# Row scatters issued two at a time inside the next group, and other PSUM banks, in a chained attention and expert kernel

## The chip, the cores and the metric

The kernel runs on one core of a Trainium2 chip. Its engines are TensorE (PE, with PEld for its weight loads), VectorE (DVE), ScalarE (ACT), GpSimd (POOL) and SyncE (SP), which only issues DMA here. The metric is the device time in microseconds. Before the change it is 1347.3 us, the median of three runs (1346.11 to 1347.62).

## The reference, cut to what matters

```
def reference(**kwargs):
    attn_out = _attn_ref(...)                 # pooled-key attention, 8 batches, 8 heads, 576 x 64
    x = attn_out.transpose(0, 2, 1, 3).reshape(4608, 512)
    x = _moe_ref(x, expert_emb, tau, w1, w2)  # each token to one of 8 experts
    return _moe2_ref(x, w1, w2, w3, w_out)

def _moe2_ref(x, w1, w2, w3, w_out):          # 4608 tokens, d_model 512, d_ff 1024
    a = x @ w1
    b = x @ w2
    h = a * b @ w3
    return (h @ w_out).astype(np.float32)
```

All is float32. The change is in the last function, the last stage of the kernel, and at its seam to the experts. The kernel has multiplied w3 and w_out into one 1024 x 512 matrix earlier, which is `wph` and `wpl` here.

## The kernel before, in words

Every float32 product is made of three products of rounded halves: a value is cast to a high half (ScalarE), the low half is the difference (VectorE or GpSimd), and `mm3` or `product` multiplies high by high, high by low and low by high. Operands in the profile end in h and l for that reason.

The expert stage (class `Moe`) sorts tokens by expert into 43 slots of 128 rows. 36 blocks always run. The rest are in nested conditional code (`single`, line 1533 ff., the branch is line 1541); each engine reads the number of used slots and skips what isn't needed. Here 37 blocks run, so one conditional block is entered and the others are skipped. Block j puts its output product in PSUM bank 5, 6 or 0 by `j % 3` (`mm2`, line 1515 ff.).

The last stage (class `Moe2`) works on the tokens in five groups: the first 512 tokens as the plain group, then four groups of 1024. Its weights w1 and w2 are read in 8 blocks, once for every group, as `w32` tiles of 512 KB from DRAM (`wload`, line 1678), two buffers.

- Plain group: `plain(k)`, k from 0 to 7, makes two products of 12 matmuls each into two PSUM banks, multiplies them and splits the result. Then `outp` makes four output tiles of 128 rows (24 matmuls each), ScalarE copies them to SBUF (line 1999), and four row scatters follow.
- Each later group: `pair(k)`, k from 8 g to 8 g + 7, treats 2 x 512 tokens in the manner of Strassen's scheme: 7 products of 6 matmuls, so 42 matmuls a pair. It needs sums of the weights, which GpSimd makes two pairs ahead (`wsums`, four operations, lines 1686 to 1689), and splits the next pair's weights in three pieces (`wpieces`, line 1713): ScalarE casts all three, VectorE makes the low half of two, and GpSimd that of the middle one. After these the load of the weights three pairs ahead is issued, which takes the buffer that the pieces just read.
- After the fourth pair of a group come 8 output products whose results ScalarE copies to the tiles o0 to o7 (line 2018); after the eighth come 8 more, which VectorE adds to them (line 2032). Between the latter the tokens of the next group are prepared (`prep`, `step`, `flip_in`). Then all 8 tiles are scattered, except that the last group scatters each tile as soon as it is summed.
- `scatter` (lines 1905 to 1915) is a one-element memset and one indirect DMA, both on GpSimd: 128 rows of 512 values go to the rows that `idx` names. `idx[g]` is filled by `flip_out` (line 1742) while group g - 1 runs.

The order on each engine is that of the Python code (`manual_schedule`): instructions are issued as the loops call them, and each waits on semaphores for its operands and for the buffers that it overwrites. PSUM has 8 banks of 128 x 512 values; a name `b0` to `b7` is one bank with one buffer. Pair k uses banks 0 to 2 if k is even and 3 to 5 if it is odd.

Of the kernel before, what the change touches and what calls it, by code (L numbers as in the profile page):

```python
# [10 lines left out]
I32 = mybir.dt.int32  # L11
# [5 lines left out]
P = 128  # L17
# [6 lines left out]
NT = N // P  # L24
# [37 lines left out]
def psum(c, bank, name):  # L62
    pool = c.psw if bank == 6 else c.ps
    return pool.tile([P, 512], F32, tag=f"b{bank}", name=name, bufs=1)
# [48 lines left out]
def mm3(nc, out, a, b, first, last):  # L113
    nc.tensor.matmul(out, a[0], b[0], start=first, stop=False)  # L114
    nc.tensor.matmul(out, a[0], b[1], start=False, stop=False)  # L115
    nc.tensor.matmul(out, a[1], b[0], start=False, stop=last)  # L116


class Fillers:
# [6 lines left out]
    def run(self, n):  # L126
        while n > 0 and self.q:
            self.q.pop(0)()
            n -= 1
# [1158 lines left out]
class Moe:  # L1288
# [226 lines left out]
    def mm2(self, j):  # L1515
        c, nc = self.c, self.c.nc
        hT = self.hT.pop(j)
        py = psum(c, (5, 6, 0)[j % 3], "py")
        for k in range(8):
            wh, wl = self.s2[k // 2]  # L1520
            mm3(nc, py, hT[k], (wh[:, k % 2, :], wl[:, k % 2, :]), k == 0, k == 7)
        self.py[j] = py
# [103 lines left out]
class Moe2:  # L1626
# [102 lines left out]
    def flip_out(self, g, ch):  # L1729
        nc = self.c.nc  # L1730
        y = self.y.pop((g, ch))
        T = self.st().rearrange("p (q t n) -> p q t n", q=4, t=2)
        for t in range(2):
            nc.vector.transpose(  # L1734
                T[:, :, t].rearrange("p q (k i) -> p q k i", k=4),
                y[:, t, :DM].rearrange("p (k q i) -> p q k i", k=4, q=4),
            )
        nc.sync.dma_start(out=self.c.scr2[ch], in_=T.rearrange("p q t n -> p q (t n)"))
        if ch == 0:
            self.idx[g] = self.wpool.tile([P, 8], I32, tag="idx", name="idx", bufs=2)  # L1740
        to = self.idx[g][:, 2 * ch:2 * ch + 2] if g == 0 else self.idx[g].rearrange("p (h c) -> p c h", h=2)[:, ch]
        nc.vector.tensor_copy(to, y[:, :, DM])

# [79 lines left out]
    def plain(self, k):  # L1823
        c, nc = self.c, self.c.nc
        h, l = self.wh.pop(k)
        p = []
        for u in range(2):
            pp = psum(c, 2 * (k % 2) + u, "pab")
            for a in range(4):
                s = (2 * u + a // 2, slice(a % 2 * P, a % 2 * P + P))  # L1830
                mm3(
                    nc, pp, (h[:, s[0], s[1]], l[:, s[0], s[1]]), tuple(x[:, a, :] for x in self.x01),
                    a == 0, a == 3,
                )
            p.append(pp)
        if k + 1 < self.PLAIN:
            self.wsplit(k + 1)
            self.wload(k + 3)
        sa = self.tmp("pa", 2)
        nc.scalar.copy(sa, p[0])  # L1840
        nc.vector.tensor_tensor(sa, sa, p[1], op=ALU.mult)
        hi, lo = (x[:, k // 4 * 512:k // 4 * 512 + 512] for x in self.abtile(k % 4))
        nc.scalar.copy(hi, sa)
        nc.vector.tensor_tensor(lo, sa, hi.bitcast(F32), op=ALU.subtract)
# [50 lines left out]

    def outp(self, g, t, fs, base):
        c, nc = self.c, self.c.nc
        po = psum(c, (0, 1, 2, 6, 7, 0, 6, 7)[t], "po")
        for n, f in enumerate(fs):
            ah, al = self.abtile(f % 4)  # L1900
            s = slice(base(f, t), base(f, t) + P)
            mm3(nc, po, (ah[:, s], al[:, s]), (c.wph[:, f, :], c.wpl[:, f, :]), n == 0, n == len(fs) - 1)
        return po
# [63 lines left out]
    def run(self, pool):  # L1967
        c, nc = self.c, self.c.nc
        self.pool = pool
        self.todo = None  # L1970
        c.wph = pool.tile([P, 8, DM], F32R, name="wph")
        c.wpl = pool.tile([P, 8, DM], F32R, name="wpl")
        for k in range(self.PLAIN):
            self.plain(k)
            if k < 4:
                self.split_wp(k)
            if k < 2:
                self.load_wp(k + 2)
            if 3 <= k <= 6:
                self.flip_out(1, k - 3)  # L1980
            if 2 <= k <= 5:
                self.load_y(1, k - 2)
            if k == 5:
                self.flip_in(1, 0)
            if k == 6:
                self.flip_in(1, 1)
                self.wsums(8)
        self.flip_in(1, 2)
        pr = [self.prep(1, ch) for ch in range(3)]
        pr[0][0]()  # L1990
        pr[1][0]()
        self.wsplit(8)
        self.wload(10)
        for t in range(4):
            po = self.outp(0, t, range(8), lambda f, t: f // 4 * 512 + t * P)
            for i in self.ORDER[0][t]:
                self.step(0, i, pr)
            self.acc[t] = o = self.partial(t)
            nc.scalar.copy(o, po)
        for t in range(4):  # L2000
            self.scatter(0, t, self.acc[t])
        for g in range(1, self.PAIRS + 1):
            more = g < self.PAIRS
            for f in range(8):
                self.pair(8 * g + f, f < 7)
                if more:
                    if f in (1, 3, 5, 6):
                        self.flip_out(g + 1, (1, 3, 5, 6).index(f))
                    if f in (0, 2, 4, 5):
                        self.load_y(g + 1, (0, 2, 4, 5).index(f))  # L2010
                    if f >= 5:
                        self.flip_in(g + 1, f - 5)
                if f == 3:
                    self.finish()
                    for t in range(8):
                        po = self.outp(g, t, range(4), lambda f, t: t * P)
                        self.acc[t] = self.partial(t)
                        nc.scalar.copy(self.acc[t], po)
            if more:
                pr = [self.prep(g + 1, ch) for ch in range(3)]  # L2020
                pr[0][0]()
                pr[1][0]()
            self.finish()
            po = {}
            for t in range(8):
                po[t] = self.outp(g, t, range(4, 8), lambda f, t: t * P)
                if more:
                    for i in self.ORDER[1][t]:
                        self.step(g, i, pr)
                for x in ((), (0,), (1, 2), (3,), (4,), (5,), (6,), (7,))[t] if more else (t,):  # L2030
                    o = self.acc[x]
                    nc.vector.tensor_tensor(o, po[x], o, op=ALU.add)
                    if not more:
                        self.scatter(g, x, o)
            for t in range(8 if more else 0):
                self.scatter(g, t, self.acc[t])

    ORDER = (
        ("abuc", "defg", "hijw", ""),
# [152 lines left out]
```

## Time and profile before

| | |
|---|---|
| median of three runs | 1347.3 us |
| the profiled execution | 1343.8 us |
| its span, first to last instruction | 1342.0 us |
| mean granted TensorE clock | 0.951 |
| PE busy | 1226.2 us (91%), 6124 matmuls |
| DVE busy | 883.3 us (66%) |
| POOL busy | 567.8 us (42%) |
| ACT busy | 496.5 us (37%) |

The last stage runs from 752.5 us of the span to its end. Busy time of PE counts matmuls that overlap their successors, so a stop shows as idle time of PE only in the waits and the timeline. The granted clock is a share of 2.4 GHz; 0.5 is 1.2 GHz. Times in rows count from the span's start.

### The profile page before, as it was taken

The numbers are of one execution on the slowest core, as the hardware profiler recorded it, in microseconds if no ns is written. First come the engines' busy times: TensorE is split into PE (matmuls) and PEld (weight loads), VectorE is DVE, ScalarE is ACT, GpSimd is POOL, SyncE is SP. The second block draws the span as 40 slices with busy tenths as digits, with TensorE's granted clock in tenths as the row PEclk, the third lists the DMA queues.
The fourth block names the chain that finished last, engine by engine and source line by source line (L and its number), as shares of the span: only waits on it lengthen the run. The fifth ranks groups of instructions, "written<-read, shape, count | busy, mean of one in ns | idle before, by whom it ended". The sixth has DMA issues, their size and how long they took to land. (4 is left out here: it accounts for less than half of the span.)

```text
span 1342.0 us, 19906 instructions
## 1 busy us (share of the span) xinstructions
PE 1226.2 (91%) x6124; PEld 964.9 (72%) x6124; DVE 883.3 (66%) x1706; ACT 496.5 (37%) x897; POOL 567.8 (42%) x705
## 2 busy tenths in 40 slices
PE   7788789899799988989898898999999999999996
PEld 6565666677677766767676686788778777787885
DVE  5999998866476586566574375728664864686262
ACT  4655455432232232233231343434334433444330
POOL 2675666622042133122232138525842663376222
PEclk9779899999999989989898999999999999999998
DMA  9999996568988878778974273315221431332001
GB/s 244 253 236 255 248 245 204 196 188 251 282 255 263 232 244 248 233 209 253 265 211 131 78 235 85 115 36 157 94 95 58 131 126 63 110 102 87 16 16 63
DMA packets 115215, 228.66 MB, mean 170 GB/s; under 512 B 11720, under 2 KB 73160, under 8 KB 115088
## 3 DMA queue, kind: packets, MB, share of 16 engines
q1 hardware_dynamic: 105824, 197.75, 50.8%
q0 software_dynamic: 8832, 28.92, 6.7%
q8 instruction: 50, 0.82, 0.3%
q14 instruction: 77, 0.63, 0.2%
q10 hardware_dynamic: 432, 0.55, 0.1%
HBM read 292.39 MB, written 72.40 MB: 272 GB/s over the span
## 5 line engine op out<-in xcount | busy, mean ns | idle before, releaser
L1483 DVE SCALAR_TENSOR_TENSOR hTl<-U,hTh 128x128 fp32r<-128x128 f32 x288 | 81.2, 344 | 112.3 <-ACT hTh L1481 75.4
L115 PE MATMUL hp<-w1l,xTh 128*128 128x512 f32 x296 | 124.8, 422 | 19.0 <-DVEq L1379 15.9
L114 PE MATMUL hp<-w1h,xTh 128*128 128x512 f32 x296 | 124.1, 419 | 15.1 <-ACT w1h L1359 11.6
L1529 POOL DMA_INDIRECT ys<-y,sidx x37 | 37.5, 1013 | 201.9 <-DVE y L1528 138.5
L116 PE MATMUL hp<-w1h,xTl 128*128 128x512 f32 x296 | 122.1, 413 | 0.0
L116 PE MATMUL py<-w2h,hTl 128*128 128x512 f32 x296 | 118.1, 399 | 3.4 <-DVE hTl L1483 3.4
L1481 ACT ACTIVATE hTh<-U 128x512 fp32r<-128x512 f32 x72 | 45.3, 631 | 204.7 <-DMA U<-scr 109.0
L114 PE MATMUL py<-w2h,hTh 128*128 128x512 f32 x296 | 118.3, 400 | 2.6 <-ACTq L1385 2.5
L115 PE MATMUL py<-w2l,hTh 128*128 128x512 f32 x296 | 118.1, 399 | 1.0 <-DVEq L1385 1.0
L1713 DVE TENSOR_TENSOR wgl<-sum,wgh 128x1024 fp32r<-128x1024 f32 x32 | 44.4, 1388 | 109.3 <-ACT wgh L1709 109.3
L116 PE MATMUL po<-wph,abl 128*128 128x512 f32 x288 | 112.9, 392 | 0.8 <-DVE abl L1858 0.6
L115 PE MATMUL po<-wpl,abh 128*128 128x512 f32 x288 | 112.3, 390 | 0.0
L114 PE MATMUL po<-wph,abh 128*128 128x512 f32 x288 | 112.2, 390 | 0.0
L1811 PE MATMUL pst<-xsh,wgh 128*128 128x512 f32 x256 | 103.8, 405 | 3.2 <-ACT pc L1879 2.1
L1811 PE MATMUL pst<-xsl,wgh 128*128 128x512 f32 x256 | 102.9, 402 | 0.4 <-DVE xsl L1801 0.4
L1811 PE MATMUL pst<-xsh,wgl 128*128 128x512 f32 x256 | 102.6, 401 | 0.0
L1713 POOL TENSOR_TENSOR wgl<-w,wgh 128x512 fp32r<-128x512 f32 x32 | 44.9, 1405 | 127.2 <-ACT wgh L1709 125.4
L115 PEld LDWEIGHTS hp<-w1l,xTh 128*128 128x128 f32 x296 | 59.6, 202 | 39.7 <-DVEq L1379 20.9
L114 PEld LDWEIGHTS hp<-w1h,xTh 128*128 128x128 f32 x296 | 59.3, 200 | 31.7 <-ACT w1h L1359 13.4
L1857 ACT CAST abh<-pa 128x512 fp32r<-128x512 f32 x32 | 19.9, 621 | 150.3 <-DVE pa L1890 150.3
L1686 POOL TENSOR_TENSOR sum<-w 128x256 f32<-128x256 f32 x32 | 28.9, 904 | 101.0 <-DMA w<-wq 74.0
L116 PEld LDWEIGHTS hp<-w1h,xTl 128*128 128x128 f32 x296 | 59.7, 202 | 13.4 <-DVE xTl L76 0.4
(300 smaller groups left out, 3143.1 us busy)
## 6 DMA issues: line engine op xcount, KB each, us to landing
w2r<-in_moe_w_dram SPq DMA_DIRECT2D x152, 512.0 KB
w1r<-in_moe_w_dram SPq DMA_DIRECT2D x150, 512.0 KB
scr<-T SPq DMA_DIRECT2D x34, 768.0 KB
U<-scr SPq DMA_DIRECT2D x136, 192.0 KB
w<-wq SPq DMA_DIRECT2D x40, 512.0 KB
yin<-ys SPq DMA_DIRECT2D x36, 256.5 KB
qs<-in_q_dram SPq DMA_DIRECT2D x16, 576.0 KB
kv<-in_k_dram SPq DMA_DIRECT2D x32, 288.0 KB
```

Of the source, the lines that this page charges most:

```text
L114: nc.tensor.matmul(out, a[0], b[0], start=first, stop=False)
L115: nc.tensor.matmul(out, a[0], b[1], start=False, stop=False)
L116: nc.tensor.matmul(out, a[1], b[0], start=False, stop=last)
L1481: nc.scalar.activation(h4, u, ACTF.Relu)
L1483: nc.vector.scalar_tensor_tensor(l4[:, k], u[:, k], 0.0, h4[:, k].bitcast(F32), op0=ALU.max, op1=ALU.subtract)
L1529: nc.gpsimd.indirect_dma_start(out=self.ys, out_offset=bass.IndirectOffsetOnAxis(ap=c.sidx[:, j:j + 1], axis=0), in_=y, in_offset=None, bo ...
L1686: g.tensor_tensor(s[:, 0], b12, b11, op=ALU.subtract)
L1713: eng.tensor_tensor(l[:, s], src, h[:, s].bitcast(F32), op=ALU.subtract)
L1811: self.c.nc.tensor.matmul(out, ws[wi], x[xi], start=first and i == 0 and n == 0, stop=i == 1 and n == 2, skip_group_check=True,)
L1857: nc.scalar.copy(hi, pr)
```

## The change

The scatters of a group are no longer issued at its end. They are put in a list, `late`, and after each pair of the next group the first two of the list are issued: four pairs for eight scatters, two for the plain group's four. The row numbers `idx` get a third buffer. The last group's own scatters stay as they are.

The first plain block writes PSUM banks 6 and 7 in place of 0 and 1 (later even blocks still 0 and 1). The plain group's four output tiles are in banks 4 to 7 in place of 0, 1, 2 and 6. Expert blocks from number 36 on, the conditional ones, put their output product in bank 5 in place of 5, 6 or 0.

```diff
     def mm2(self, j):
-        py = psum(c, (5, 6, 0)[j % 3], "py")
+        py = psum(c, (5, 6, 0)[j % 3] if j < NT else 5, "py")
...
     def flip_out(self, g, ch):
-            self.idx[g] = self.wpool.tile([P, 8], I32, tag="idx", name="idx", bufs=2)
+            self.idx[g] = self.wpool.tile([P, 8], I32, tag="idx", name="idx", bufs=3)
...
     def plain(self, k):
-            pp = psum(c, 2 * (k % 2) + u, "pab")
+            pp = psum(c, (6 if k == 0 else 2 * (k % 2)) + u, "pab")
...
     def outp(self, g, t, fs, base):
-        po = psum(c, (0, 1, 2, 6, 7, 0, 6, 7)[t], "po")
+        po = psum(c, (4, 5, 6, 7)[t] if g == 0 else (0, 1, 2, 6, 7, 0, 6, 7)[t], "po")
...
     def run(self, pool):
             self.acc[t] = o = self.partial(t)
             nc.scalar.copy(o, po)
-        for t in range(4):
-            self.scatter(0, t, self.acc[t])
+        late = [(0, t) for t in range(4)]
         for g in range(1, self.PAIRS + 1):
             more = g < self.PAIRS
             for f in range(8):
                 self.pair(8 * g + f, f < 7)
+                for x in late[:2]:
+                    self.scatter(*x, self.acc[x[1]])
+                del late[:2]
                 if more:
...
                     if not more:
                         self.scatter(g, x, o)
-            for t in range(8 if more else 0):
-                self.scatter(g, t, self.acc[t])
+            late = [(g, t) for t in range(8 if more else 0)]
```

## Rows read from the trace of the kernel before

**Rows 1.** Waits of PE from 745 us on: total us, times, longest.
```profile
PE pst L1811 <- POOL wgl L1713: 10.0, 4, 3.8
PE pab L114 <- DVEq L1541: 3.5, 1, 3.5
...
PE pst L1811 <- ACT o L1999: 1.1, 1, 1.1
...
PE pst L1811 <- DVE xsl L1801: 0.4, 1, 0.4
```

**Rows 2.** Stretches of PE: from:to, length, busy (count), clock, DMA share, GB/s.
```profile
752.52:759.69 7.17, 7.17 (x25) 0.76 0.49 149
765.28:770.78 5.50, 5.50 (x26) 1.00 0.60 191
820.47:832.24 11.77, 10.26 (x43) 1.00 0.22 86
832.24:848.65 16.41, 12.66 (x44) 0.79 0.31 93
890.67:900.33 9.66, 9.66 (x43) 1.00 0.26 87
900.34:909.97 9.63, 9.63 (x44) 1.00 0.22 76
961.33:974.92 13.59, 11.51 (x44) 0.87 0.32 111
1214.94:1228.51 13.57, 11.49 (x43) 0.87 0.21 54
```

**Rows 3.** POOL in order of time, 943 to 990: start, us, ..., [idle before].
```profile
949.07 0.98 POOL L1908 DMA_INDIRECT out_dram<-o,idx  x1 [0.16 <-issue]
...
958.48 0.96 POOL L1908 DMA_INDIRECT out_dram<-o,idx  x1 [0.22 <-issue]
959.46 0.76 POOL L1686 TENSOR_TENSOR sum<-w 128x256 f32<-128x256 f32 x1
...
962.72 1.26 POOL L1713 TENSOR_TENSOR wgl<-w,wgh 128x512 fp32r<-128x512 f32 x1
967.86 0.80 POOL L1686 TENSOR_TENSOR sum<-w 128x256 f32<-128x256 f32 x1 [3.88 <-DMA w<-wq]
...
970.82 1.47 POOL L1713 TENSOR_TENSOR wgl<-w,wgh 128x512 fp32r<-128x512 f32 x1
975.91 0.74 POOL L1686 TENSOR_TENSOR sum<-w 128x256 f32<-128x256 f32 x1 [3.62 <-DVE pb L1892]
```

**Rows 4.** POOL in order of time, 820 to 846.
```profile
826.88 1.68 POOL L1908 DMA_INDIRECT out_dram<-o,idx  x1 [0.22 <-issue]
...
831.12 0.75 POOL L1686 TENSOR_TENSOR sum<-w 128x256 f32<-128x256 f32 x1
...
834.86 1.70 POOL L1713 TENSOR_TENSOR wgl<-w,wgh 128x512 fp32r<-128x512 f32 x1
```

**Rows 5.** ACT in order of time, 952 to 958.
```profile
955.15 0.63 ACT L1709 CAST wgh<-w 128x512 fp32r<-128x512 f32 x1
```

**Rows 6.** POOL in order of time, 1216 to 1240.
```profile
1225.13 1.29 POOL L1713 TENSOR_TENSOR wgl<-w,wgh 128x512 fp32r<-128x512 f32 x1
1230.26 1.13 POOL L1686 TENSOR_TENSOR sum<-w 128x256 f32<-128x256 f32 x1 [3.84 <-DVE abl L1858]
```

**Rows 7.** PE in order of time, 748.5 to 754.3.
```profile
752.52 0.47 PE L114 MATMUL pab<-xah,wgh 128*128 128x512 f32 x1 [3.51 <-DVEq L1541]
```

**Rows 8.** Line 1541's queue instructions, 744.9 to 752.6: ns min/median/max, first and last start.
```profile
L1541 PEldq COMPARE_BRANCH  x2: 193/1834/3475, 745.1 to 749.4; - x2
...
L1541 DVEq EVENT_SEMAPHORE  x2: 21/21/21, 752.4 to 752.5; - x2
```

**Rows 9.** DVE in order of time, 748 to 755.
```profile
753.57 1.23 DVE L1713 TENSOR_TENSOR wgl<-w,wgh 128x1024 fp32r<-128x1024 f32 x1 [3.71 <-ACT wgh L1709]
```

**Rows 10.** PE in order of time, 819.5 to 825.
```profile
824.02 0.50 PE L1811 MATMUL pst<-xsl,wgh 128*128 128x512 f32 x1 [0.40 <-DVE xsl L1801]
```

## The prediction

> **What bounds the kernel now.** I read the waits of TensorE over the last stage first, because the matrix engine is busy nearly throughout there and only what stops it can be won. Of its stops the large ones have two causes: four waits for the low half of a weight piece that GpSimd (POOL) writes, 10.0 us together with 3.8 us the longest, and one wait of 3.5 us for VectorE's queue ahead of the stage's first product [rows 1]. A third, 1.1 us, is for a copy out of PSUM, and 0.4 us follows it for an operand.
>
> Then I cut the stage into stretches that hold the same work, so that a stop and the slow clock behind it show as one difference [rows 2]. A pair of blocks (42 matmuls) takes 9.66 and 9.63 us where nothing stops it. Pair 9, the second after the plain group, takes 16.41 us; pair 17, the second of the next group, takes 13.59; pair 33 takes 13.57, and pair 25 between them is like them (three such pairs, the first and last shown). The first plain block takes 7.17 us where a later one takes 5.50. The granted clock says why these are longer than their stop: its mean is 0.76, 0.79 and 0.87 of full in the long stretches and 1.00 in the others. Each of these long stretches has a stop of 2.1 us or more at or just before its start (the three like ones (10.0 - 3.8) / 3 each); pair 8, whose stops are the 1.1 and 0.4 us, kept 1.00. So what a large stop costs is the stop and a stretch at 1.2 instead of 2.4 GHz behind it.
>
> Third, GpSimd's own order around such a stop [rows 3]. Eight scatters stand between the weight sums of one pair and those of the next: the first starts at 949.07 and the last at 958.48, and at 959.46 the sums start with no idle time at all before them. The piece that TensorE waits for starts at 962.72 and ends at 963.98; the pair that needs it had started at 961.33. GpSimd was simply still issuing scatters.
>
> **The scatters moved.** Removed from the start of each group: eight scatters, 949.07 to 959.44, 10.4 us of GpSimd, at three boundaries, and four after the plain group, which end just before the sums at 831.12 [rows 3, 4]. None is deleted; each comes back two at a time behind the piece that GpSimd writes in the first four pairs (in two pairs after the plain group).
>
> What is late next at a boundary: the sums can't start before the scatters' old place, 949.0, and must not start later than 959.46, which bounds the gain on that side at nothing. They take from 959.46 to 962.72, so from 949 they would be done near 953. The piece itself also needs ScalarE's cast, which starts at 955.15 and takes 0.63 [rows 5]. So it would start at about 955.8 and end at 957.1 by the 1.26 us of its row, 4.2 us before the pair starts at 961.33. The same kernel shows this case already: pairs 12 and 13 stand in the middle of a group, where no scatter stands ahead of their sums, and take 9.66 and 9.63 us [rows 2]. I take pair 13 as the model of pairs 17, 25 and 33: 3 x (13.59 - 9.63) with 13.57 for the last gives 11.9 us. Pair 9 after the plain group: 16.41 - 9.63 = 6.8 us. There the four scatters end and the sums start at 831.12, the piece starts at 834.86 and ends at 836.56, while pair 9 starts at 832.24. Four scatters at 1.34 us (below) are 5.4 us; begun that much earlier, it ends at about 831.2, 1 us ahead.
>
> What the scatters cost in their new place: after a piece GpSimd is idle 3.62 to 3.84 us until the next weights land [rows 3, 6], because the load of these waits for that very piece to free their buffer. One scatter is 1.34 us from start to start in the run of eight (949.07 to 958.48 over seven steps). Two are 2.7 us and fit. The bound on the other side is the slowest of all, 1.68 us [rows 4]; two such, with the 0.3 us each that memset and waiting add to the row's 0.96 or 0.98 (949.07 to 959.46 over eight), are 4.0 us, 0.4 over the hole. Behind the hole the piece still has room: pair 17's next piece ends at 972.29 against a pair start at 974.92 (2.6 us), and in the last group 1226.42 against 1228.51 (2.1 us) [rows 2, 3, 6]. So 0.4 us late reaches nobody, and I cost this at nothing. If that room were gone, each microsecond would be a stop of TensorE in three pairs of each of four groups (the fourth pair is followed by output products). The scatters' data now move while a weight load does; the hole was 3.88 us in pair 17, where the code issues two token loads of the same size right behind the weight load, and 3.62 us in the next pair, where it issues none there [rows 3]. So traffic of this size costs 0.3 us, within the same room.
>
> One page of the Trainium skill speaks against the new place. SBUF — State Buffer, section "SBUF: two separate sides", says that VectorE in some modes locks GpSimd out while it must write descriptors, and gives 620 ns growing to about 3100 ns. By the page's factor two scatters would be near 7 us, an estimate from that page. The trace here agrees only in kind: its slowest scatter is 0.7 us over the usual one (1.68 against 0.96) [rows 3, 4]. The sum stands without the page; the third rival below is the same mechanism, priced from rows.
>
> A third buffer of the row numbers goes with it: the numbers of a group are then still read while those of the group after next could be written. With three buffers VectorE's write waits for older scatters than now, so nothing is added. The output tiles are overwritten in the fourth pair's product block; the last two scatters are issued ahead of that, and the copy into tile 6 comes after six output products. No cost.
>
> **Other PSUM banks.** The first plain block's products move from banks 0 and 1, which the skipped tail blocks of the expert stage may have used, to 6 and 7; and the expert outputs of tail blocks stay on bank 5. TensorE's first product now starts at 752.52 after 3.51 us of idling, released by VectorE's queue at the end of the conditional code [rows 7]. There VectorE's queue goes on at 752.4; TensorE's own last branch starts at 749.4 and takes 0.2 [rows 8]. With a bank that no conditional block touches, the wait for VectorE has no ground, and TensorE may start when its own queue is through: I take 749.8, 2.7 us earlier. Bounds: nothing gained if another wait has the same releaser, 2.9 if it starts at 749.6. With an idle time of 0.8 us instead of 3.5 I also expect the full clock, 7.17 - 5.50 = 1.7 us. The second block needs its weights' low part, which VectorE ends at 753.57 + 1.23 = 754.80 [rows 9], unmoved; the first block would end at 749.8 + 5.5 = 755.3, so this holds by 0.5 us. Later steps of the plain group follow the products and move with them.
>
> The plain group's outputs on banks 4 to 7 free bank 2 for pair 8, whose second product waits 1.1 us for the copy [rows 1]; but its next matmul at 824.02 waits for VectorE's operand [rows 10], which the banks don't touch. So the start of that wait moves and its end doesn't: nothing. The upper bound is pair 8's whole excess, 11.77 - 9.66 = 2.1 us.
>
> **Sum.** 11.9 + 6.8 + 2.7 + 1.7 = 23.1 us. The profiled execution took 1343.8 us (span 1342.0), so it would take 1320.7. The three timed runs have a median 3.5 us above it; I carry the difference over: 1347.3 - 23.1 = 1324.2 us.
>
> **Rivals.** (1) The first product still waits for VectorE's queue, because of another operand written under the same semaphore. For: the row names VectorE's queue and no tile; against: ScalarE's and VectorE's parts of that block's operands were made long before. Then 2.7 and 1.7 are lost: 1328.6 us. (2) The stops go but the slow clock comes anyway. For: the rows show stop and slow clock together and not which brings which; against: in this stage 1.00 held in every stretch without a large stop [rows 2]. Then only idle time is won, 2.7 + 10.0 = 12.7 [rows 1]: 1334.6 us. (3) The scatters are much slower between the blocks than at the boundary, locked out by VectorE or queued behind each other, so that sums and piece of the next pair come late. Its place is the hole of 3.6 us; it starts to cost when two scatters take 3.6 + 2.1 = 5.7 us. The sign turns at stops of 1.9 us in three pairs of four groups (12 x 1.9 = 23), two scatters of 7.6 us, 3.8 each. At stops of 2.1 us each pair would also lose the clock as pair 17 does, 12 x 3.96 = 47.5, less 23.1: 1371.7 us. Against: the slowest of the rows is 2.0 us with its memset. (4) The change doesn't do what it says: the sums wait at 949 for something else that ends near 959, and only the work is reshuffled: 1347 us. Against: sums that directly follow other sums at mid-group.
>
> **How the numbers follow.** Forecast 0.78, (1) 0.12, (2) 0.05, (3) 0.03, (4) 0.02. The range 1320.5 to 1332 holds the forecast with pair 8's 2.1 us won on one side and, on the other, (1) and up to 0.25 us of new waiting in each of 12 pairs; (2) to (4) are left out. Under 0.2% (2.7 us) a measurement here can't be told from no change. Faster 0.95, same 0.02, slower 0.03.
>
> **What would show it.** Right: pairs 9, 17, 25 and 33 near 9.7 us with a granted clock of 1.00; no scatter between the last sums of a group and the first of the next; two scatters inside each hole; TensorE's first product about 1 us after its last expert product. Wrong: a wait of TensorE for the piece in pairs 10, 11, 18 or 19; scatters over 2 us; the first product still released by VectorE's queue; or the 824.02 wait grown, which would mean that its operand's chain does not move with the plain group.

## The result, and the profile after

The changed kernel takes 1324.3 us (median of four runs, 1322.66 to 1329.95), against 1346.7 us (1342.73 to 1347.62) for the kernel before on the same chip; the ratio is 0.9861, with an interval of 0.9824 to 0.9898. The forecast was 1324.2 us.

The profiled execution took 1324.6 us, with a span of 1322.8 us. I call "the stage" what lies between the end of the experts' last product and the end of the span; that product ends for its successor 0.23 us after its start, the usual step of TensorE. After the change the last expert product starts at 752.94, so the stage is 1322.8 - 753.17 = 569.6 us. In the profile before that product starts at 748.61:

```profile
748.61 0.40 PE L116 MATMUL py<-w2h,hTl 128*128 128x512 f32 x1
```

The same sum gives 593.2 us there. The stage became 23.6 us shorter, the execution only 19.2 us: the expert part ahead of it was 4.3 us longer this time.

First, TensorE's waits from 748 us on (total us, times, longest), the answer to [rows 1]:

```profile
PE pst L1811 <- ACT pc L1879: 1.5, 3, 0.5
PE pst L1811 <- DVE xsl L1801: 0.9, 1, 0.9
PE po L116 <- DVE abl L1858: 0.7, 1, 0.7
PE pab L114 <- PEq L1541: 0.6, 1, 0.6
PE pst L1811 <- ACT xsh L1796: 0.2, 1, 0.2
```

The four waits for GpSimd's piece, 10.0 us, have no row any more, and the wait for VectorE's queue has become 0.6 us for TensorE's own. The wait for the copy out of PSUM (1.1 us) is gone too, but the one for `xsl` has grown from 0.4 to 0.9 and one of 0.2 for `xsh` has come.

Second, the stretches that answer to [rows 2]: the first plain block, then pairs 8, 9, 17, 25 and 33 (from:to, length, busy, clock, DMA share, GB/s):

```profile
753.92:759.49 5.57, 5.57 (x24) 1.00 0.10 31
820.31:831.64 11.33, 10.25 (x43) 1.00 0.09 9
831.64:841.28 9.64, 9.64 (x43) 1.00 0.54 170
954.03:963.66 9.63, 9.63 (x43) 1.00 0.46 128
1076.56:1086.22 9.66, 9.66 (x43) 1.00 0.45 128
1199.64:1209.29 9.65, 9.65 (x43) 1.00 0.20 58
```

Pairs 9, 17, 25 and 33 now take what pairs 12 and 13 took before (9.66 and 9.63 us [rows 2]) and still take, at a granted clock of 1.00.

Third, TensorE at the two places where banks were changed, the seam and pair 8 (start, us, engine, line, operation, [idle before]), the answer to [rows 7, 10]:

```profile
752.94 0.39 PE L116 MATMUL py<-w2h,hTl 128*128 128x512 f32 x1
753.92 0.50 PE L114 MATMUL pab<-xah,wgh 128*128 128x512 f32 x1 [0.59 <-PEq L1541]
...
823.42 0.50 PE L1811 MATMUL pst<-xsl,wgh 128*128 128x512 f32 x1 [0.89 <-DVE xsl L1801]
```

Fourth, GpSimd in order of time, behind the plain group and at the next boundary, the answer to [rows 3, 4]:

```profile
838.29 1.29 POOL L1713 TENSOR_TENSOR wgl<-w,wgh 128x512 fp32r<-128x512 f32 x1
...
841.05 1.33 POOL L1908 DMA_INDIRECT out_dram<-o,idx  x1 [0.22 <-issue]
...
848.32 1.30 POOL L1713 TENSOR_TENSOR wgl<-w,wgh 128x512 fp32r<-128x512 f32 x1
...
948.56 1.33 POOL L1713 TENSOR_TENSOR wgl<-w,wgh 128x512 fp32r<-128x512 f32 x1 [4.04 <-ACT wgh L1709]
...
954.31 0.74 POOL L1686 TENSOR_TENSOR sum<-w 128x256 f32<-128x256 f32 x1 [1.98 <-DVE pa L1890]
...
959.06 1.28 POOL L1713 TENSOR_TENSOR wgl<-w,wgh 128x512 fp32r<-128x512 f32 x1
...
960.52 0.98 POOL L1908 DMA_INDIRECT out_dram<-o,idx  x1 [0.16 <-issue]
...
961.81 0.96 POOL L1908 DMA_INDIRECT out_dram<-o,idx  x1 [0.22 <-issue]
...
965.16 0.75 POOL L1686 TENSOR_TENSOR sum<-w 128x256 f32<-128x256 f32 x1 [2.39 <-DMA w<-wq]
...
969.93 1.48 POOL L1713 TENSOR_TENSOR wgl<-w,wgh 128x512 fp32r<-128x512 f32 x1
```

The piece for pair 17 ends at 949.89, 4.1 us before the pair starts at 954.03 (before: 963.98 in a pair that had started at 961.33). Two scatters stand in the hole behind each piece. The hole behind the piece for pair 18, from its end at 960.34 to the sums at 965.16, has grown from 3.6 to 4.8 us, and what follows is closer: the piece from 969.93 ends at 971.41, 2.2 us before pair 19 starts at 973.65. The narrowest place is behind the plain group: the piece from 838.29 ends at 839.58 and pair 10 starts at 841.28, 1.7 us; the next one, from 848.32, ends 1.5 us before pair 11 starts at 851.15.

### The profile page after: what moved, and what is told of

It reads as the page before. It is cut to its first block, busy times and chain, and to the rows that moved or that the text cites. A ratio compares the mean times of both kernels' runs of the same rounds, so it can differ in the third digit from the quotient of the medians.

```text
span 1322.8 us, 19897 instructions
## 1 busy us (share of the span) xinstructions
PE 1208.6 (91%) x6124; PEld 948.9 (72%) x6124; DVE 877.7 (66%) x1706; ACT 496.2 (38%) x897; POOL 569.8 (43%) x705
## 5 line engine op out<-in xcount | busy, mean ns | idle before, releaser
L115 PE MATMUL hp<-w1l,xTh 128*128 128x512 f32 x296 | 122.1, 412 | 21.5 <-DVEq L1379 16.8
L114 PE MATMUL hp<-w1h,xTh 128*128 128x512 f32 x296 | 120.6, 408 | 14.1 <-ACT w1h L1359 10.9
L116 PE MATMUL hp<-w1h,xTl 128*128 128x512 f32 x296 | 119.2, 403 | 0.0
L114 PEld LDWEIGHTS py<-w2h,hTh 128*128 128x128 f32 x296 | 56.4, 191 | 27.8 <-ACTq L1385 13.5
L115 PEld LDWEIGHTS py<-w2l,hTh 128*128 128x128 f32 x296 | 56.5, 191 | 16.1 <-DVEq L1385 1.7
```

## The experiments

Diffs are against the changed kernel unless the text says otherwise. Each time the kernel before ran on the same chip too; its median there is called "before". A stage or a pair is from the one profiled execution of its kernel.

### One part at a time

`scatters_only` keeps the late scatters and puts the three PSUM choices back:

```diff
-        py = psum(c, (5, 6, 0)[j % 3] if j < NT else 5, "py")
+        py = psum(c, (5, 6, 0)[j % 3], "py")
...
-            pp = psum(c, (6 if k == 0 else 2 * (k % 2)) + u, "pab")
+            pp = psum(c, 2 * (k % 2) + u, "pab")
...
-        po = psum(c, (4, 5, 6, 7)[t] if g == 0 else (0, 1, 2, 6, 7, 0, 6, 7)[t], "po")
+        po = psum(c, (0, 1, 2, 6, 7, 0, 6, 7)[t], "po")
```

> The scatters moved (with the third buffer of row numbers), all PSUM banks as before. Theory, GpSimd's order made the four large stops: pairs 9, 17, 25 and 33 come to 9.6 to 9.7 us at granted clock 1.00, TensorE's waits for the middle piece vanish, while the first plain block keeps its 3.5 us wait and its 7.2 us. Saved 6.8 + 11.8 = 18.6 us: 1328 us by the clock of the timed runs. Rival, the banks of the plain group's outputs have a part in pair 9's stop: pair 9 stays above 12 us and the saving is near 11.8: 1335 us.

Measured: 1328.4 us (nine runs; before 1342.7), ratio 0.9908, 0.9882 to 0.9933; the stage 575.3 us. Its stretches, the first plain block and pairs 9 and 17:

```profile
748.22:755.29 7.07, 7.07 (x25) 0.77 0.45 152
827.79:837.42 9.63, 9.63 (x43) 1.00 0.58 172
950.72:960.35 9.63, 9.63 (x43) 1.00 0.46 142
```

So the scatters alone win all of the pairs and nothing of the seam. The stage is 17.9 us shorter than in the first profile before, and 14.3 us shorter than in the second one (`before_again`, 589.6 us, below). The time agrees with the 1328 us expected by luck: the saving by medians is 14.3 us and not 18.6, and the kernel before was 4.6 us faster here than the 1347.3 us that I had started from.

`first_banks_only` leaves the scatters at the group's end and the outputs on their old banks, and keeps the new banks of the first plain block and of the conditional expert blocks. Against the kernel before:

```diff
-        py = psum(c, (5, 6, 0)[j % 3], "py")
+        py = psum(c, (5, 6, 0)[j % 3] if j < NT else 5, "py")
...
-            pp = psum(c, 2 * (k % 2) + u, "pab")
+            pp = psum(c, (6 if k == 0 else 2 * (k % 2)) + u, "pab")
```

> Only the first plain block's banks (6 and 7) and the tail blocks' bank (5). Theory: TensorE idles about 0.6 us before its first product instead of 3.5, the block takes 5.5 us at clock 1.00 instead of 7.2, and the stage moves forward whole: 4.5 us, 1342 us; the four stops for the middle piece stay at 3.8 and 2.1 us. Rival, the operands of the first group after it come at fixed times: pair 8 grows from 11.8 towards 16 us and the time stays at 1346.7.

Measured: 1335.0 us (ten runs, on the same chip), ratio 0.9955, 0.993 to 0.9979, where I had put 1342; the stage 585.2 us, 8.0 less than in the profile before. The seam gave its part, 4.5 us: the first block took 5.57 us and waited 0.59. The other 3.5 us are in pairs whose banks are the old ones: 1.6 in pair 17, 1.2 in pair 9 (15.17 us) and 0.7 in pair 8 (11.12 us). Pairs 17 and 25:

```profile
953.71:965.69 11.98, 9.90 (x44) 1.00 0.27 88
1078.62:1092.22 13.60, 11.52 (x43) 0.87 0.30 108
```

Both pairs stop for the piece alike (2.1 us more than their busy time), but in pair 17 the clock stayed at 1.00. Against the second profile before (`before_again`) the stage is 4.4 us shorter, which is the seam's part alone.

`first_banks_py_kept` is the same with the conditional blocks back on banks 5, 6 and 0, so that only the first plain block has new banks. Against the kernel before:

```diff
-            pp = psum(c, 2 * (k % 2) + u, "pab")
+            pp = psum(c, (6 if k == 0 else 2 * (k % 2)) + u, "pab")
```

> The first plain block on banks 6 and 7, but the tail blocks keep banks 5, 6 and 0 by their number, so that the skipped block 37 would have written bank 6. Theory, the wait is for whatever a skipped block might have done to that bank: TensorE still idles about 3.5 us, released by VectorE's queue, block 7.2 us. Rival, leaving banks 0 and 1 is enough: 0.6 us and 5.5 us.

Measured: 1340.3 us in one run, the stage 589.1 us. TensorE's first product:

```profile
753.16 0.79 PE L114 MATMUL pab<-xah,wgh 128*128 128x512 f32 x1 [3.56 <-DVEq L1541]
```

The wait is whole. New banks for the first block don't do as long as a skipped conditional block names one of them, bank 6: the edit of the conditional blocks is needed too. That this edit alone would not do either was not tried; the code speaks for it, because the conditional blocks' first products (`mm1`) name bank 1, which the first plain block would then still write.

`outp_banks_only` keeps nothing but the plain group's outputs on banks 4 to 7. Against the kernel before:

```diff
-        po = psum(c, (0, 1, 2, 6, 7, 0, 6, 7)[t], "po")
+        po = psum(c, (4, 5, 6, 7)[t] if g == 0 else (0, 1, 2, 6, 7, 0, 6, 7)[t], "po")
```

> Only the plain group's outputs moved to banks 4 to 7. Theory: pair 8's wait for the PSUM copy goes, the wait for VectorE's operand ends at the same place behind the start of the pair: pair 8 takes 11.3 to 11.8 us, the rest is unchanged. Rival, the copy was what counted: pair 8 falls by the 1.1 us of that wait to 10.7 us or less.

Measured: 1339.5 us in one run, the stage 590.7 us, pair 8 at 10.94 us. That lies between what the two theories allowed, and pair 8 also takes 11.12 and 11.32 us in the two kernels above, which don't have these banks; its length alone decides nothing. The rows do, TensorE's first, then the one of VectorE that it waits for, and last the same operation in the kernel before:

```profile
821.17 0.50 PE L1811 MATMUL pst<-xsl,wgh 128*128 128x512 f32 x1 [0.89 <-DVE xsl L1801]
```

```profile
819.75 1.36 DVE L1801 TENSOR_TENSOR xsl<-sum,xsh 128x1024 fp32r<-128x1024 f32 x1 [2.54 <-ACT xsh L1796]
```

```profile
822.62 1.35 DVE L1801 TENSOR_TENSOR xsl<-sum,xsh 128x1024 fp32r<-128x1024 f32 x1 [2.53 <-ACT xsh L1796]
```

The wait for the copy is gone here as in the changed kernel, and the wait for `xsl` is the same 0.89 us that it is there. In this kernel and in the one before the product starts 0.05 to 0.06 us after `xsl` is done (821.17 after 821.11, 824.02 after 823.97), with the copy in the way or without it. So the banks move the start of that wait, and `xsl` sets its end. When `xsl` is done varies by itself: 2.84 to 3.50 us into pair 8 in the five kernels and executions with the old output banks, 2.66 to 3.58 us in the seven with the new ones and the early weight load.

### More scatters at a time

`four_at_once` and `eight_at_once` issue four, or all eight, behind the first pairs' pieces:

```diff
-                for x in late[:2]:
+                for x in late[:4]:
                     self.scatter(*x, self.acc[x[1]])
-                del late[:2]
+                del late[:4]
```

> As the changed kernel, but four scatters behind each of the first two pairs of a group (all four of the plain group behind one). Theory, what counts is whether the scatters fit GpSimd's idle time behind the piece and the room of the next piece: two more are 2.6 us, the idle time left in the changed kernel's holes is 1.4 to 2.4 us and the next piece's room 1.7 to 3.3, so it is 0.2 to 1.2 us over a hole and within the room. No stop of TensorE: pairs 9 to 11, 17 to 19 stay at 9.6 to 10.4 us, stage 569 to 571 us. Rival, each scatter beside a pair holds that pair up (port or DMA): the first two pairs grow by more than 1 us each, stage over 575 us.

> As the changed kernel, but all of a group's scatters behind its first pair. Theory: eight are 10.4 us, 7.8 more than now, over the hole's remaining 2 us by 5.8 us; the piece behind (room 3.1 to 3.3 us) comes 2.5 us late, so pairs 18, 26 and 34 show a stop of about 2.2 us each, with or without a slow clock behind it 2.2 to 4 us; after the plain group (four) no stop. Stage 570 + 7 to 12 = 577 to 582 us. Rival, it is enough that the scatters leave the boundary: no stop, stage 570 us.

Measured: four 1325.2 us, ratio 0.9896 (0.9855 to 0.9938); eight 1321.8 us, ratio 0.9876 (0.9838 to 0.9914), before 1339.8. The stages are 573.4 and 572.6 us, 2 to 4 us longer than with two (569.6, and 570.6 in `after_again`). The intervals of the two ratios overlap; in the profiled executions the expert part differs by more than the stages do (the first plain product starts at 742.12 with eight and at 752.69 with four). For eight the theory held in kind and not in size: there is a wait for the piece again, at 1.0 us instead of about 2.2, and the stage is 4 us below the 577 to 582 that I had put. The wait:

```profile
PE pst L1811 <- POOL wgl L1713: 2.9, 3, 1.0
```

For four it missed: I had seen room for them, and pairs 18 and 26 took 11.56 us. The waits name another releaser there, ScalarE's copy `pc`, longest 1.6 us; there is none for the piece. Pair 18 of `four_at_once`:

```profile
962.24:973.80 11.56, 9.93 (x44) 1.00 0.56 205
```

What ScalarE waits for just then:

```profile
967.91 0.58 ACT L1876 COPY pb<-pst 128x512 f32<-128x512 f32 x1 [2.56 <-DVE abl L1858]
```

VectorE's operation that releases it:

```profile
964.30 0.68 DVE L1858 TENSOR_TENSOR abl<-pa,abh 128x512 fp32r<-128x512 f32 x1
964.90 2.92 DVE L1858 TENSOR_TENSOR abl<-pb,abh 128x512 fp32r<-128x512 f32 x1
```

And GpSimd at that time:

```profile
965.13 0.74 POOL L1686 TENSOR_TENSOR sum<-w 128x256 f32<-128x256 f32 x1
965.83 0.74 POOL L1687 TENSOR_TENSOR sum<-w 128x256 f32<-128x256 f32 x1
966.54 0.73 POOL L1688 TENSOR_TENSOR sum<-w,sum 128x256 f32<-128x256 f32 x1
967.35 1.07 POOL L1689 TENSOR_TENSOR sum<-w,sum 128x256 f32<-128x256 f32 x1
```

A split of the same shape took 0.68 us a moment earlier and 2.92 us here; it ended at 967.82, 0.5 us behind GpSimd's third sum. Pair 26 shows the same (2.92 us), and in pair 33 it is the first split (2.87 us, the pair 10.90). So a second theory: the scatters push the sums onto VectorE's split, and that collision stops TensorE, not lateness. The Trainium skill, in SBUF — State Buffer, section "Who interferes with whom", says that a VectorE instruction with two inputs in SBUF contends with a GpSimd instruction that reads SBUF; split and sums are both of that kind, and these rows agree (0.68 against 2.92 us).

The two theories part on what a further delay does: by lateness it makes the stop longer, by collision it takes it away. `four_then_wait` adds ten memsets of one element behind the four scatters, on GpSimd:

```diff
-                for x in late[:2]:
+                for x in late[:4]:
                     self.scatter(*x, self.acc[x[1]])
-                del late[:2]
+                    if x is late[:4][-1]:
+                        for _ in range(10):
+                            self.c.nc.gpsimd.memset(self.mark, 0.0)
+                del late[:4]
```

> Four scatters at a time as in the kernel of that name, and behind them ten memsets of one element on GpSimd, about 1 us, so that the weight sums start later still. Theory collision: the sums now start behind VectorE's split, which falls back from 2.9 to 0.7 to 1.2 us, and pairs 18 and 26 take 10.4 us or less instead of 11.56; stage 570 to 572 us. Rival lateness (the sums and their piece were simply too late with four): 1 us more of it makes pairs 18 and 26 some 12.5 us, with a wait for the piece, and the stage 576 us or more.

Measured: 1325.2 us in one run, the stage 568.2 us, 5.2 less than without the memsets. Pair 18, at 965.69:

```profile
965.69:975.35 9.66, 9.66 (x43) 1.00 0.54 203
```

VectorE's second split in it:

```profile
968.35 0.72 DVE L1858 TENSOR_TENSOR abl<-pb,abh 128x512 fp32r<-128x512 f32 x1
```

GpSimd in it:

```profile
969.31 1.41 POOL L2009 MEMSET mark<- 1x1 f32 x10
970.72 0.74 POOL L1686 TENSOR_TENSOR sum<-w 128x256 f32<-128x256 f32 x1
...
973.83 1.30 POOL L1713 TENSOR_TENSOR wgl<-w,wgh 128x512 fp32r<-128x512 f32 x1
```

1.4 us of useless work made pair 18 shorter by 1.9 us, and the rival had forecast it longer by 0.9. It is one execution, but three pairs in it say the same: pair 26 went from 11.56 to 9.66 us with its split at 0.72, and pair 33 from 10.90 to 9.63 with 0.69. The piece ends at 975.13, though, 0.2 us before pair 19 starts (0.1 us at the narrowest place): by then lateness is next in line.

`three_at_once` has 3 in both places.

```diff
-                for x in late[:2]:
+                for x in late[:3]:
```

> The scatters of a group stand three at a time behind the piece of the next group's first pairs, instead of two. Theory collision (the stops of four at once came from GpSimd's weight sums, shifted by the scatters until they run beside VectorE's split): three scatters are some 3.9 us against a hole of 4.2 to 4.9 us, so the sums still start with the landed weights; the split stays at 0.7 to 1.2 us and pairs 18 and 26 take 10.0 to 10.4 us as with two; stage 569 to 571 us. Rival lateness (every scatter added makes the sums one scatter later): sums 0.5 to 1 us later, pairs 18 and 26 take 10.5 us or more, stage 571 to 573 us.

Measured: 1330.5 us in one run with a late expert end (its first plain product starts at 759.79), the stage 569.7 us, pair 18 at 9.94 us:

```profile
969.91:979.85 9.94, 9.94 (x44) 1.00 0.52 173
```

The changed kernel's split in its pair 18, and the pair itself in the changed kernel's two executions (the second is `after_again`, below):

```profile
966.45 1.23 DVE L1858 TENSOR_TENSOR abl<-pb,abh 128x512 fp32r<-128x512 f32 x1
```

```profile
963.66:973.65 9.99, 9.93 (x43) 1.00 0.45 154
```

```profile
969.49:979.98 10.49, 9.95 (x44) 1.00 0.47 148
```

Three cost no more than two here; the split took 1.24 us, so the collision is there in its small form, as in the changed kernel. The numbers lie just outside what the theory gave (0.7 to 1.2 us for the split, 10.0 to 10.4 for the pair). As two scatters alone let pair 18 vary from 9.99 to 10.49 us, one run with 9.94 is weak evidence against the rival's 10.5; `four_then_wait` is what decides between the two.

### Pair 8, and both kernels again

`load_after_flip` issues the weight load of the plain group's end behind the first token load, on which TensorE's operand `xsl` depends:

```diff
         self.wsplit(8)
-        self.wload(10)
         for t in range(4):
             po = self.outp(0, t, range(8), lambda f, t: f // 4 * 512 + t * P)
             for i in self.ORDER[0][t]:
                 self.step(0, i, pr)
+            if t == 0:
+                self.wload(10)
```

> As the changed kernel, but the load of the weights of pair 10 is issued behind the reads of the fourth token chunk of group 1, which wait behind it in SyncE's queue now. Theory, these reads are what VectorE's operand in pair 8 hangs on: they start some 3 us earlier, the wait in pair 8 (0.9 + 0.2 us, pair 8 at 11.3) goes and pair 8 takes under 10.2 us, stage 568.5. Rival, the reads wait for their buffers anyway: pair 8 stays at 11 to 11.8 us; the later load may make pair 9 wait instead.

Measured: 1318.1 us, ratio 0.9852 (0.9811 to 0.9894) to the kernel before, and the stage 568.8 us. Pair 8 has no wait for `xsl` any more, which is done 1.5 us into the pair, and is under the 10.2 us expected, and neither of the two pairs behind it stops for a piece:

```profile
812.75:822.58 9.83, 9.83 (x43) 1.00 0.07 10
822.58:832.21 9.63, 9.63 (x43) 1.00 0.57 169
832.21:842.09 9.88, 9.88 (x43) 1.00 0.42 151
```

`before_again` is the kernel before, once more, to see whether its stops are the same in another execution.

> The kernel before once more, for a second trace. Theory, the stops are set by the order and recur: idle 3.7 us before the first plain product, stops of 3.8 and 2.1 us in pairs 9, 17, 25 and 33. Whether the slow clock follows each of them recurs is open: with it pairs 17, 25 and 33 take 13.6 us, without it 11.9. Rival, the stops are chance and differ in place.

Measured: 1337.2 us in one run, the stage 589.6 us, against 593.2. The waits are there in the same places (10.0 us in four for the piece, 3.6 for VectorE's queue). Pairs 17 and 25:

```profile
957.04:969.04 12.00, 9.90 (x44) 1.00 0.26 87
1081.68:1095.26 13.58, 11.49 (x43) 0.87 0.35 106
```

Again a pair with the stop and without the slow clock; in the first profile of the same kernel pair 17 had it [rows 2].

`after_again` is the changed kernel once more and `load_after_flip_2` the later load, on one chip:

> The changed kernel once more, beside a version that loads a weight piece later, on one chip. Theory (the mechanism holds in every execution): no wait of TensorE for the piece, pairs 9, 17, 25 and 33 within 0.1 us of 9.65, pair 8 at 10.9 to 11.8 us, stage 569 to 571 us, 1318 to 1325 us in all. Rival (what one execution showed was its own): one of the stops of 2 us or more is back, stage 573 us or more.

> The changed kernel with the load of the weight piece after the first token load behind the plain group, instead of ahead of both. Theory (pair 8's second wait hangs on the tokens' load behind that weight load): pair 8 at 9.8 to 10 us and the stage 1 to 2 us shorter than in the changed kernel on the same chip, so 0.1% in time, less than these runs can tell; nothing else moves. Rival (the later weight load makes the next piece late): a wait for the piece in pair 9 or 10 and the stage as long as before or longer.

Measured: 1329.3 us (six runs, 1325.27 to 1331.7), ratio 0.987 (0.9838 to 0.9902), and 1324.5 us (six, 1321.87 to 1328.17), ratio 0.9838 (0.9806 to 0.987), before 1344.8. Both intervals lie below 1. The stages are 570.6 and 569.3 us. Pairs 8 and 17 in the first:

```profile
826.38:837.46 11.08, 10.17 (x43) 1.00 0.07 9
959.82:969.49 9.67, 9.67 (x44) 1.00 0.45 137
```

and pair 8 in the second:

```profile
824.34:834.54 10.20, 10.00 (x43) 1.00 0.09 10
```

The large stops stay away in both traced executions of the changed kernel. Its absolute time did not hold: I had put 1318 to 1325 us. The later load wins 0.9 to 1.5 us in pair 8 (10.20 us against the 9.8 to 10 that I had put for the second time), less than the 4.8 us between the two medians, whose ratios overlap; the traces show the pair, and the times don't tell the kernels apart.

## Why the prediction was right

**The terms.** Pairs 17 and 33 went from 13.59 and 13.57 to 9.63 and 9.65 us, and pair 25, at 9.66, like them: 11.8 us (predicted 11.9). Pair 9: 16.41 - 9.64 = 6.8 us (6.8). TensorE's idle time at the seam: 3.51 - 0.59 = 2.9 us (2.7, bound 2.9). The clock of the first block: 7.17 - 5.57 = 1.6 us (1.7). Pair 8: 0.4 us (0, bound 2.1). Together 23.5 us of 23.6 in the stage. The sum fits this one pair of profiles; what of it is sure to come stands below. `scatters_only` puts the first two terms on the scatters, and `first_banks_only` with `first_banks_py_kept` puts the next two on the pair of bank edits.

**The rivals.** Rival (1), another operand behind the same queue, fell with the 0.59 us row. Rival (2), the slow clock without the stops, fell: 1.00 in every stretch above. (Only the last 34.2 us of the span, with 12 us of idle time, are at 0.87, as they were at 0.88 before.) Rival (3) needed two scatters of 5.7 us; they took 0.98 and 0.96, the slowest 1.33 behind the boundary at 841.05. The starving of descriptor writing that the Trainium skill describes (SBUF — State Buffer, "SBUF: two separate sides"; about 3100 ns) shows in no scatter of these runs: the longest in the kernels that issue them between the blocks is 1.45 us, in `after_again`. The prediction's "near 7 us" is about twice those 3100 ns with the memsets and waits, and not the page's factor, which would give more; the sum did not use it. Rival (4) fell with the pieces' new times.

**Where a size was off.** The step "so 0.4 us late reaches nobody" was right in its end and too narrow in its working. I priced the scatters and left out the sums behind them. The sums ahead of pair 18's piece, at 954.31 to 959.06, took 4.8 us; before, at 967.86 to 970.82, they had taken 3.0 [rows 3]. VectorE's splits and low half (954.96 to 958.49) run beside them now; that these are what stretches the sums is read from the overlap and was not tried by itself. The hole behind that piece grew by 1.2 us, where I had put 0.3 for the traffic. The room that I gave as 2.1 to 2.6 us is 1.5 to 1.7 behind the plain group. Two and three scatters lie within it; with four, the collision that I hadn't considered decides, and 0.1 to 0.2 us of room are left once it is gone.

For pair 8 the step "the start of that wait moves and its end doesn't" holds in this sense: the banks move the start, and the operand sets the end, by a chain that the banks don't touch; `load_after_flip` shows that it depends on when the tokens are loaded. I had named a longer wait there as a sign that the operand's chain didn't move with the plain group, and that was a badly chosen sign: it became longer because the wait ahead of it went, while its end, counted from the pair's start, came earlier (823.42 - 820.31 = 3.1 us against 824.02 - 820.47 = 3.6). The 0.4 us won lie within what pair 8 varies by between kernels without these banks (11.12 to 11.77); with them it took 10.94 to 11.86 us.

**What the good figure hides.** Some 1.6 us in each of pairs 17, 25 and 33 (13.59 - 12.00) are the slow clock behind the stop, and it is not sure to come: it was missing in one of the three pairs in `before_again`, `first_banks_only` and `outp_banks_only`, and in two of them in `first_banks_py_kept`, each time after a stop of the same length. Pair 9 took 15.01 to 16.15 us in these four kernels, against the 16.41 that I had used, after a stop of 3.7 to 3.8 us in all of them. By the stages of two executions each, 593.2 and 589.6 against 569.6 and 570.6, the change is worth 19 to 23.6 us, and I priced it from the upper case. The two ratios, 0.9861 and 0.987, are 18.7 and 17.5 us; mine was 0.9829, near the edge of the first interval and outside the second. The hit to 0.1 us is luck in part, through the spread of the expert part, at which no edit aimed: the first plain product starts anywhere from 742.12 (`eight_at_once`) to 760.06 (`after_again`). Why that part varies was not tried, and it stays open.

## What to carry to other kernels

Work that nobody waits for still delays what its engine must do next: put it behind the last thing of the stretch that somebody needs, and count the room there with the neighbour's work, not only with its own length. A stop that names an odd releaser (a queue, a copy on a third engine) is worth following one step back, since a delay can cure a collision, as in `four_then_wait`, and not a lateness. Where conditional code precedes a stage, try to give the stage's first products PSUM banks that no skipped block names; here that took 2.9 us of idle time from TensorE.

## What the runs showed of the hardware that was not expected

- The slow clock behind a stop is not sure: with stops of 2.1 us in the same pair of the same code, the granted clock was 1.00 in one execution (12.00 us for pair 17) and 0.87 in another (13.59). What decides was not settled.
- One VectorE split of one shape took 0.68 to 0.72 us alone, 1.23 when GpSimd's sums had begun before it, and 2.87 to 2.92 when they began 0.2 us after it and ran back to back. In the last case the first three sums took 0.73 to 0.76 us each, no longer than elsewhere, so VectorE paid nearly all of it (the fourth took 1.07 us).
- The scatters now land later, a median of 4.5 us from issue (3.9 in `after_again`) instead of 2.7, and nobody waits for that.
